# B's output projection in four column groups, and one row of its weights in sixteen transfers

## The chip, the core and the metric

The kernel runs on one core of a Trainium2 chip. The metric is the device time of one execution in microseconds (us), as the median of several runs. A core has four engines that compute (TensorE for matmuls, VectorE, ScalarE, GpSimd) and SyncE, which here only issues transfers. In the profile they are PE (PEld is its weight load), DVE, ACT, POOL and SP. Each engine works through its own list of instructions in order. Transfers (DMA) are issued by SyncE and ScalarE and carried out by sixteen DMA engines beside the computing ones.

## What is computed

Two attention layers for one new token, A and B, with their own inputs, each with 32 heads of 128 and a model width of 512. A looks at the whole cache of 16384 positions, B at its last 4096. For each side:

```python
q = (lambda x, *d: x.transpose(*d))((x @ wq).reshape(B, Sq, Hq, Dh), 0, 2, 1, 3)
...
scores = jnp.einsum("bhqd,bhkd->bhqk", q, k) * (Dh ** -0.5)
p = _softmax(scores, axis=-1)
o = jnp.einsum("bhqk,bhkd->bhqd", p, v)
return (lambda x, *d: x.transpose(*d))(o, 0, 2, 1, 3).reshape(B, Sq, Hq * Dh) @ wo
```

The output is the two results side by side, 1024 numbers in bfloat16: A's 512, then B's 512. The last step, `@ wo`, takes a vector of 4096 (32 heads by 128) to 512.

## The kernel before

Nearly all of the 352 MB read are K and V. The caches are cut into twenty steps, sixteen of two heads of A and four of eight heads of B (B at steps 0, 7, 13 and 19, so the last step is B's). For each step SyncE loads a K tile and a V tile of 8 MB; VectorE multiplies K by q and sums over the 128 elements of a head (`scores_prod`, `scores_tree`); ScalarE does the exponentials; TensorE multiplies the probabilities with V (`pv`) one step later. K has two buffers, V one. The order of the instructions on each engine is the order of the program text (`tc.manual_schedule`), with one loop over the steps (L446) and a hand-written ending (L473 to L489).

The last step's tiles hold other things too. At the last step (L452) a K buffer is taken for A's `wo` (4 MB, L454) and for the first half of the last V (L455); after the loop the V buffer is taken for the second half of the last V (L474) and B's `wo` (L475). `wo` lies in memory as 4096 rows of 512; a partition holds 32 consecutive rows, called r here, of 512 numbers. `load_wo` (L152) loads B's `wo` in five pieces of 16, 8, 4, 3 and 1 of those 32, each over all 128 partitions (L156, L157). All these loads are issued by SyncE, one behind the other.

The ending then runs: A's output vector is turned (`permute_o`), projected with 32 matmuls of 512 columns (`project_out_rows`, L380) and stored from ScalarE's queue (L388). B's last softmax follows, then the two halves of its last V (`pv_columns`, L354, 128 matmuls each), each followed by a product on VectorE (L362); then `permute_o(B)`, which leaves the vector as `OpB`, 128 partitions by 32. `project_out_columns` (L390) has `wo` as the weights: for each piece of the load, each block of 128 output columns and each r one matmul with 128x128 weights and one column of `OpB` as the moving side (L397). The result has the output columns on partitions, one partial sum for each piece and block. VectorE adds the five partial sums (L403), TensorE transposes the 128x4 result (L407), VectorE copies it to bfloat16 (L409), and SyncE stores four rows of 128 (L410).

Each transfer reports its end on a semaphore. The framework hands out eight of these for the queues of SyncE and ScalarE together, in turn, and puts the waits that it takes to be needed ahead of an issue, on the issuing engine.

Of the kernel before, what the change touches and what calls it, by code (L numbers as in the profile page):

```python
# [9 lines left out]
F32 = mybir.dt.float32  # L10
BF16 = mybir.dt.bfloat16
P = 128
ACT = mybir.ActivationFunctionType
ALU = mybir.AluOpType
AX = mybir.AxisListType

HQ, DH = 32, 128
CH = 128
# [7 lines left out]
def kernel(  # L26
# [14 lines left out]
    nc = tc.nc  # L41
# [4 lines left out]
    DN = A_wo.shape[1]  # L46
# [8 lines left out]
    one = ctx.enter_context(tc.tile_pool(name="one", bufs=1))  # L55
    ps_t = ctx.enter_context(tc.tile_pool(name="ps_t", bufs=2, space=bass.MemoryType.PSUM))
    ps_s = ctx.enter_context(tc.tile_pool(name="ps_s", bufs=2, space=bass.MemoryType.PSUM))
# [3 lines left out]
    def kslot(name):  # L61
        return kring.tile([P, 2 * CH, DH], BF16, tag="kring", name=name)

    def vslot(name):
        return vring.tile([P, 2 * CH, DH], BF16, tag="vring", name=name)

    identf = singles.tile([P, P], F32, tag="identf")
# [6 lines left out]
    A, B = _Side(), _Side()  # L74
# [36 lines left out]
    def new_k(T):  # L111
        K[T] = kslot("kt")

    def load_k(T, u=None):
        s, g = steps[T]
        if s is A:
            nc.sync.dma_start(
                out=K[T][:, :, :].rearrange("p l d -> p (l d)"),
                in_=a_pair(A_k_cache, g).rearrange("p l d -> p (l d)"),
            )  # L120
        else:
            for v in (0, 1) if u is None else (u,):
                nc.sync.dma_start(
                    out=K[T][:, v * CH : (v + 1) * CH, :].rearrange("p l d -> p (l d)"),
                    in_=b_window(B_k_cache, 2 * g + v),
                )
# [13 lines left out]
    def load_v_half(T, u, dst):  # L140
        nc.sync.dma_start(  # L141
            out=dst.rearrange("p l d -> p (l d)"), in_=b_window(B_v_cache, 2 * steps[T][1] + u)
        )

    def load_wq(s, W):
        s.wq_t = W
        nc.sync.dma_start(
            out=W.rearrange("p a b -> p (a b)").rearrange("p (c f) -> p c f", c=KC),
            in_=s.wq.rearrange("(p c) f -> p c f", c=KC),
        )  # L150

    def load_wo(s, W, pieces):  # L152
        s.wo_t = W.rearrange("p a b -> p (a b)").rearrange("p (r f) -> p r f", r=HQ)
        src = s.wo.rearrange("(p r) f -> p r f", r=HQ)
        r = 0
        for n in pieces:  # L156
            nc.sync.dma_start(out=s.wo_t[:, r : r + n, :], in_=src[:, r : r + n, :])  # L157
            r += n

    def make_masks(s):  # L160
        nc.vector.tensor_reduce(out=s.mask[:, :], in_=by_head(s, identf[:, :]), axis=AX.X, op=ALU.add)
        n = 8 * s.groups // s.nh
        nc.vector.tensor_copy(
            s.rows[:, :, :, :], s.mask[:, :].unsqueeze(1).unsqueeze(3).broadcast_to([P, n, s.nh, 4])
        )
        for v in range(s.parts):
            w = 32 * s.groups
            block = identf[:, v * w : (v + 1) * w].rearrange("p (g r) -> p r g", g=s.groups)
            nc.vector.tensor_reduce(
                out=s.sel[:, v, :], in_=block[:, 0 : 4 * s.nh, :], axis=AX.X, op=ALU.add  # L170
            )
# [10 lines left out]
    def spread_x(s, flat):  # L182
        s.xb = flat[:, 0 : s.nh * KC * P].rearrange("p (h c m) -> p h c m", h=s.nh, c=KC)
        nc.vector.memset(s.xb, 0.0)
        turn_x(s)
        for j in range(s.nh):
            dst = s.xb[:, j, :, :]
            if s is A:
                dst = dst.rearrange("p c (h i) -> p c h i", h=s.nh)[:, :, j, :]
            else:  # L190
                dst = dst.rearrange("p c (i h) -> p c i h", h=s.nh)[:, :, :, j]
            nc.vector.tensor_copy(dst, s.xT[:, :].unsqueeze(2).broadcast_to([P, KC, P // s.nh]))
# [194 lines left out]
        nc.scalar.copy(row[:, :], ps[:, :])  # L387
        nc.scalar.dma_start(out=out[0, 0:1, 0:DN], in_=row[:, :])  # L388

    def project_out_columns(s, pieces):  # L390
        nf, npc = DN // P, len(pieces)
        ps = ps_s.tile([P, npc, nf], F32, tag="sp", name="out_cols")
        r0 = 0
        for k, n in enumerate(pieces):
            for c in range(nf):
                for r in range(r0, r0 + n):
                    nc.tensor.matmul(  # L397
                        ps[:, k, c : c + 1], lhsT=s.wo_t[:, r, c * P : (c + 1) * P], rhs=s.Op[:, r : r + 1],
                        start=(r == r0), stop=(r == r0 + n - 1),
                    )  # L400
            r0 += n
        cols = one.tile([P, nf], F32, tag="cols", name="cols")
        nc.vector.tensor_reduce(  # L403
            out=cols[:, :], in_=ps[:, :, :].rearrange("p k c -> p c k"), axis=AX.X, op=ALU.add
        )
        pr = ps_t.tile([nf, P], F32, tag="tp", name="out_rows")
        nc.tensor.transpose(pr[:, :], cols[:, :], identf[:, :])  # L407
        rows = one.tile([nf, P], BF16, tag="p", name="rows")
        nc.vector.tensor_copy(rows[:, :], pr[:, :])  # L409
        nc.sync.dma_start(out=out[0, 0, DN : 2 * DN].rearrange("(c f) -> c f", c=nf), in_=rows[:, :])  # L410

    wo_pieces = (16, 8, 4, 3, 1)
    with tc.manual_schedule():
        scratch = kslot("scratch")
        x0 = 4 * KC * P
        for s in (B, A):
            s.x_row = scratch[0:1, :, :].rearrange("p a b -> p (a b)")[:, x0 : x0 + D]
            for a, b in ((0, D // 4), (D // 4, D // 2), (D // 2, D)):
                nc.scalar.dma_start(out=s.x_row[:, a:b], in_=s.x[0, 0:1, a:b])  # L419
            x0 += D  # L420
        new_k(0)
        wqt = vslot("wqt")
        load_wq(B, wqt[:, 0:CH, :])
        load_k(0, 0)
        load_wq(A, wqt[:, CH : 2 * CH, :])
        load_k(0, 1)
        make_identity(nc, identf[:, :])
        nc.vector.memset(one_f[:, :], 1.0)
        nc.vector.memset(one_b[:, :], 1.0)
        nc.vector.memset(ones_col[:, :], 1.0)  # L430
        nc.vector.memset(A.o[:, :], 0.0)
        nc.vector.memset(B.o[:, :], 0.0)
        nc.vector.tensor_copy(ident[:, :], identf[:, :])
        spread_x(B, scratch[:, :, :].rearrange("p a b -> p (a b)"))
        for s in (B, A):
            make_masks(s)
        nc.vector.memset(pick[:, :], 0.0)
        nc.vector.tensor_copy(
            pick[:, 4 : 4 + P].rearrange("h (m k) -> h m k", k=4)[:, :, 0], identf[0:HQ, 0:HQ]
        )  # L440
        spread_x(A, one.tile([P, 2 * KC * P], BF16, tag="o4", name="xbA")[:, :])
        project_q(B)
        project_q(A)
        new_k(1)
        load_k(1)
        for T in range(NT):  # L446
            if T >= 1:
                load_v(T - 1)
                if T + 1 < NT:
                    new_k(T + 1)  # L450
                    load_k(T + 1)
            if T == NT - 1:  # L452
                W = kslot("wot")
                load_wo(A, W[:, 0:CH, :], (HQ,))  # L454
                load_v_half(T, 0, W[:, CH : 2 * CH, :])  # L455
            scores_prod(T, 0)
            if T >= 1:
                un = units[T - 1]
                max_all(un)
                soft(un)  # L460
                spread_p(un)
                soft_sum(un)
                pv(un)
            scores_tree(T, 0)
            if T >= 1:
                recip(un)
                evict(un)
                columns(un)
            scores_prod(T, 1)
            scores_tree(T, 1)  # L470
            if T < NT - 1:
                unit_max(units[T])
        Z = vslot("wot")  # L473
        load_v_half(NT - 1, 1, Z[:, 0:CH, :])  # L474
        load_wo(B, Z[:, CH : 2 * CH, :], wo_pieces)  # L475
        un = units[NT - 1]
        permute_o(A)
        project_out_rows(A)
        unit_max(un)
        max_all(un)  # L480
        soft(un)
        spread_p(un, 0, CH)
        spread_p(un, CH, 2 * CH, nc.vector.tensor_scalar_mul)
        soft_sum(un)
        recip(un)
        pv_columns(un, 0, W[:, CH : 2 * CH, :])
        pv_columns(un, 1, Z[:, 0:CH, :])
        permute_o(B)
        project_out_columns(B, wo_pieces)  # L489


# [28 lines left out]
```

## Time and profile before

| | |
|---|---|
| median of 3 runs | 825.76 us (825.72 to 825.88) |
| span of the profiled execution, first to last instruction | 823.9 us |
| DVE busy | 763.9 us, 93% |
| PE busy | 202.7 us, 25% |
| ACT busy | 60.1 us, 7% |
| moved by DMA | 352.62 MB, mean 428 GB/s |
| chain that ended last, share of DMA | 82% |
| mean granted TensorE clock | 0.592 |

The span is that of the one execution that was profiled; the runs that give the median are timed without a profile and include what lies around the span. The chain that ended last is followed back from the last instruction, at each step to what released it. Times in the profile's views count from the start of the span. "Granted clock" is the share of TensorE's full clock that it was given in a stretch. In the views of instructions a line such as "L397" is a line of the kernel before, and "x16" a number of merged instructions; in the views of waits the columns are the waiting engine and line, what it waited for, us in total, times, and the longest.

### The profile page before, as it was taken

Reading aid. Unit: us, or ns where it says so; the run is one execution under the profiler, and the core shown is the slowest. Engines: PE = TensorE matmul, PEld = TensorE weight load, DVE = VectorE, ACT = ScalarE, POOL = GpSimd, SP = SyncE. Lnnn points to the kernel's source line nnn. Section 1 sums busy time; section 2 is a strip of 40 time slices with the busy share of each in tenths; the row PEclk is TensorE's granted clock in tenths of the full one; section 3 lists DMA queues with packets and bytes.
Section 4 is the critical chain, followed back from the end, with each engine's and each line's share of the span. In section 5 each row is a group of like instructions: output and inputs, shape, how many; then the busy total and the mean of one; then the engine's idle time right before and its main releaser. Section 6 shows DMA issues by size and latency. Waiting matters only on the chain.

```text
span 823.9 us, 4724 instructions
## 1 busy us (share of the span) xinstructions
PE 202.7 (25%) x1985; PEld 100.7 (12%) x1985; DVE 763.9 (93%) x353; ACT 60.1 (7%) x168; POOL 0.7 (0%) x6
## 2 busy tenths in 40 slices
PE   2702212203030303130312213030303020303175
PEld 0201100101010101010101101010101010101035
DVE  2899999999999999999999999999999999999980
ACT  0101000001010000100000000010100000000010
POOL 0000000000000000000000000000000000000000
PEclk9865656565565555565555565565656565556585
DMA  9999999999999999999999999999999999999997
GB/s 384 434 433 433 453 420 443 430 436 440 423 446 420 424 439 443 412 453 420 443 417 449 414 452 410 450 417 428 438 449 424 436 433 430 443 414 445 418 429 296
DMA packets 8107, 352.62 MB, mean 428 GB/s; under 512 B 915, under 2 KB 1046, under 8 KB 1302
## 3 DMA queue, kind: packets, MB, share of 16 engines
q1 hardware_dynamic: 8072, 352.33, 99.2%
q8 instruction: 15, 0.25, 0.1%
q14 instruction: 6, 0.05, 0.0%
q10 hardware_dynamic: 14, 0.00, 0.0%
HBM read 352.32 MB, written 0.00 MB: 428 GB/s over the span
## 4 chain that ended last, share of the span: by engine, by line
DMA 82%; PE 15%; DVE 1%; SPq 0%; issue 0%; ACTq 0%; ACT 0%; DVEq 0%
DMA vt<-in_A_v_cache_dram 65%; DMA vt<-in_B_v_cache_dram 13%; PE oA L331 11%; DMA wot<-in_B_wo_dram 4%; PE oB L331 2%; PE qp L203 2%; DMA scratch<-in_A_x_dram 2%; DVE kt L227 1%; SPq L141 0%; ACTq L419 0%; SPq L157 0%; PE out_cols L397 0%; ACT qB L207 0%; PE out_rows L407 0%; DVE rows L409 0%
## 5 line engine op out<-in xcount | busy, mean ns | idle before, releaser
L233 DVE TENSOR_TENSOR kt<-kt 128x8192 bf16<-128x8192 bf16 (+3 forms) x160 | 344.9, 2156 | 4.8
L227 DVE TENSOR_TENSOR kt<-kt,qA 128x16384 bf16<-128x16384 bf16 x32 | 277.8, 8683 | 11.0 <-DMA kt<-in_A_k_cache_dram 10.9
L331 PE MATMUL oA<-vt,pm 128*8 128x512 bf16 x1024 | 92.3, 538 | 132.1 <-DMA vt<-in_A_v_cache_dram 132.1
L227 DVE TENSOR_TENSOR kt<-kt,qB 128x16384 bf16<-128x16384 bf16 x8 | 69.4, 8680 | 6.3 <-ACT qB L207 6.3
L249 PE MATMUL sm<-identf,m 128*1 128x128 f32 x24 | 8.1, 370 | 227.3 <-DVE m L244 227.3
L331 PEld LDWEIGHTS <-pm 128*8 128x8 bf16 (+1 forms) x1216 | 37.3, 111 | 216.7 <-issue 196.3
L268 PE MATMUL sm<-one_f,Mr 1*128 1x1 f32 x48 | 12.9, 347 | 176.7 <-DVE Mr L264 147.1
L237 DVE TENSOR_REDUCE sc<-kt 128x128 f32<-128x1024 bf16 x40 | 48.8, 1220 | 2.7
L276 ACT ACTIVATE bias<-sm 128x1 f32<-128x1 f32 (+1 forms) x20 | 3.4, 172 | 420.8 <-PE sm L268 420.8
L268 PEld LDWEIGHTS sm<-one_f,Mr 1*128 1x128 f32 x48 | 11.2, 298 | 183.6 <-DVE Mr L264 152.2
L249 PEld LDWEIGHTS sm<-identf,m 128*1 128x1 f32 x24 | 1.7, 79 | 229.3 <-issue 216.2
L340 ACT ACTIVATE o<-oA,r 128x512 f32<-128x512 f32 x16 | 11.0, 688 | 220.5 <-PE oA L331 220.5
L331 PE MATMUL oB<-vt,pm 128*16 128x512 bf16 x192 | 17.2, 494 | 20.3 <-DMA vt<-in_B_v_cache_dram 16.2
L348 PE MATMUL oc<-selA,o 128*128 128x2 f32 x128 | 16.9, 254 | 12.7 <-ACT o L340 12.7
L348 PEld LDWEIGHTS oc<-selA,o 128*128 128x128 f32 x128 | 15.5, 191 | 20.8 <-ACT o L340 20.8
L297 ACT ACTIVATE pm<-p,maskA 128x256 bf16<-128x256 bf16 x32 | 14.5, 500 | 0.5
L315 PE MATMUL sm<-cs,rowsA 128*128 128x1 f32 x32 | 9.4, 362 | 14.3 <-ACT p L282 14.3
L282 ACT ACTIVATE p<-sc,bias 128x256 bf16<-128x256 f32 (+1 forms) x24 | 11.3, 470 | 0.6
L203 PE MATMUL qp<-wqt,xbA 128*128 128x512 bf16 x32 | 8.8, 444 | 6.0 <-DVE kt L227 6.0
L315 PEld LDWEIGHTS sm<-cs,rowsA 128*128 128x128 f32 x32 | 8.0, 310 | 15.7 <-ACT p L282 15.7
L203 PE MATMUL qp<-wqt,scratch 128*128 128x512 bf16 x32 | 9.9, 486 | 0.0
L362 DVE TENSOR_TENSOR OB<-ocol,r 128x4 bf16<-128x4 f32 x2 | 0.3, 161 | 10.2 <-PE ocol L358 10.2
(71 smaller groups left out, 108.1 us busy)
## 6 DMA issues: line engine op xcount, KB each, us to landing
kt<-in_B_k_cache_dram SPq DMA_DIRECT2D x8, 4096.0 KB, 29.1
vt<-in_B_v_cache_dram SPq DMA_DIRECT2D x6, 4096.0 KB, 23.3
wot<-in_B_v_cache_dram SPq DMA_DIRECT2D x2, 4096.0 KB, 22.6
wqt<-in_B_wq_dram SPq DMA_DIRECT2D x1, 4096.0 KB, 12.3
wqt<-in_A_wq_dram SPq DMA_DIRECT2D x1, 4096.0 KB
wot<-in_A_wo_dram SPq DMA_DIRECT2D x1, 4096.0 KB
wot<-in_B_wo_dram SPq DMA_DIRECT2D x1, 2048.0 KB
wot<-in_B_wo_dram SPq DMA_DIRECT2D x1, 1024.0 KB
```

Of the source, the lines that this page charges most:

```text
L203: nc.tensor.matmul(qp[:, :, :], lhsT=s.xb[:, j, c, :], rhs=wq[:, c, j, g : g + 4, :], start=(k == 0), stop=(k == n - 1),)
L227: nc.vector.tensor_tensor(out=k, in0=k, in1=s.q[:, j : j + 1, :].broadcast_to([P, CH, DH]), op=ALU.mult)
L233: nc.vector.tensor_tensor(out=k[:, :, 0:w], in0=k[:, :, 0:w], in1=k[:, :, w : 2 * w], op=ALU.add)
L237: nc.vector.tensor_reduce(out=units[T].sc[:, u * CH : (u + 1) * CH], in_=k[:, :, 0:8], axis=AX.X, op=ALU.add)
L249: nc.tensor.transpose(un.sm[0:1, v * P : (v + 1) * P], m[:, v : v + 1], identf[:, :])
L268: nc.tensor.matmul(un.sm[:, 256 + v : 257 + v], lhsT=Mr[:, v * P : (v + 1) * P], rhs=one_f[:, :], start=True, stop=True,)
L282: nc.scalar.activation(out=un.p[:, v * n : (v + 1) * n], in_=un.sc[:, v * n : (v + 1) * n], func=ACT.Exp, scale=inv, bias=bias[:, v : v + ...
L297: nc.scalar.activation(out=out, in_=in_, func=ACT.Copy, scale=mask)
L315: nc.tensor.matmul(un.sm[v * w : (v + 1) * w, 264:265], lhsT=s.rows[:, :, :, :].rearrange("p r a b -> p (r a b)"), rhs=un.cs[:, v : v + 1] ...
L331: nc.tensor.matmul(s.o[r0 : r0 + un.rows, :], lhsT=un.pm[:, l, :, :].rearrange("p a b -> p (a b)"), rhs=V[un.T][:, 4 * l : 4 * l + 4, :], ...
L340: nc.scalar.activation(out=un.osb[:, :], in_=un.s.o[:, :], func=ACT.Copy, scale=un.r[:, 0:1])
L348: nc.tensor.matmul(oc[:, 0:w], lhsT=un.osb[:, j * P : (j + 1) * P], rhs=sel[:, j, :], start=(j == 0), stop=(j == 3),)
```

## The change

`load_wo` gets an option that is used for B. With it, row r = 0 of the 32 is loaded first and by itself, in sixteen transfers of 15, 14, 13 and so on down to 1 partitions, and a last one of 8 (together 128), each partition 512 numbers or 1 KB. The first big piece is then 15 of the 32 instead of 16. The number of transfers for B's `wo` goes from 5 to 21, all on SyncE's queue, in front of B's store.

`project_out_columns` is replaced by `project_out_groups`. One column of `OpB` is now the weights (128x1) and a 128x128 block of `wo` the moving side; for each r there are four matmuls, one for each block of output columns, which write to partitions 0, 32, 64 and 96 of one PSUM tile and so go to four column groups of TensorE. All 32 r are summed in place. The tile is cleared by VectorE before. The sum over pieces, the transpose and their tiles are gone: one copy of 128x128 to bfloat16 follows, and the store takes the four partitions 0, 32, 64 and 96.

```diff
-    def load_wo(s, W, pieces):
+    def load_wo(s, W, pieces, spread=False):
...
         r = 0
+        if spread:
+            p = 0
+            for k in (*range(15, 0, -1), 8):
+                nc.sync.dma_start(out=s.wo_t[p : p + k, 0, :], in_=src[p : p + k, 0, :])
+                p += k
+            assert p == P
+            r, pieces = 1, (pieces[0] - 1, *pieces[1:])
         for n in pieces:
...
-    def project_out_columns(s, pieces):
-        nf, npc = DN // P, len(pieces)
-        ps = ps_s.tile([P, npc, nf], F32, tag="sp", name="out_cols")
-        r0 = 0
-        for k, n in enumerate(pieces):
+    def project_out_groups(s, pieces):
+        nf = DN // P
+        ps = ps_s.tile([P, P], F32, tag="sp", name="out_groups")
+        nc.vector.memset(ps[:, :], 0.0)
+        for r in range(HQ):
             for c in range(nf):
-                for r in range(r0, r0 + n):
-                    nc.tensor.matmul(
-                        ps[:, k, c : c + 1], lhsT=s.wo_t[:, r, c * P : (c + 1) * P], rhs=s.Op[:, r : r + 1],
-                        start=(r == r0), stop=(r == r0 + n - 1),
-                    )
-            r0 += n
-        cols = one.tile([P, nf], F32, tag="cols", name="cols")
-        nc.vector.tensor_reduce(
-            out=cols[:, :], in_=ps[:, :, :].rearrange("p k c -> p c k"), axis=AX.X, op=ALU.add
-        )
-        pr = ps_t.tile([nf, P], F32, tag="tp", name="out_rows")
-        nc.tensor.transpose(pr[:, :], cols[:, :], identf[:, :])
-        rows = one.tile([nf, P], BF16, tag="p", name="rows")
-        nc.vector.tensor_copy(rows[:, :], pr[:, :])
-        nc.sync.dma_start(out=out[0, 0, DN : 2 * DN].rearrange("(c f) -> c f", c=nf), in_=rows[:, :])
+                nc.tensor.matmul(
+                    ps[32 * c : 32 * c + 1, :], lhsT=s.Op[:, r : r + 1], rhs=s.wo_t[:, r, c * P : (c + 1) * P],
+                    start=(r == 0), stop=(r == HQ - 1),
+                )
+        rows = one.tile([P, P], BF16, tag="p", name="rows")
+        nc.vector.tensor_copy(rows[:, :], ps[:, :])
+        nc.sync.dma_start(
+            out=out[0, 0, DN : 2 * DN].rearrange("(c f) -> c f", c=nf),
+            in_=rows[:, :].rearrange("(c k) f -> c k f", c=nf)[:, 0, :],
+        )
...
-        load_wo(B, Z[:, CH : 2 * CH, :], wo_pieces)
+        load_wo(B, Z[:, CH : 2 * CH, :], wo_pieces, spread=True)
...
-        project_out_columns(B, wo_pieces)
+        project_out_groups(B, wo_pieces)
```

## The prediction

> **What bounds the kernel now.** I read the chain of waits first, and of it only the last 40 us, because every edit lies in the last load and the last projection. Columns: start, length, what.
>
> ```profile
> 787.87 0.54 SPq L141
> 788.41 0.05 issue
> 788.46 0.58 SPq L157
> 789.04 0.05 issue
> 789.10 0.42 SPq L157
> ...
> 790.04 30.16 DMA wot<-in_B_wo_dram
> 820.19 0.04 issue
> 820.24 0.60 PE out_cols L397 x16
> 820.84 0.02 issue
> 820.86 0.19 DVE cols L403
> 821.05 0.04 issue
> 821.09 0.39 PE out_rows L407
> ```
>
> The reader is to see that the end hangs on a transfer: SyncE issues the second half of the last V (L141) at 787.9 and all five pieces of wo (L157) right behind it, and then data flows until 820.19. Only 16 matmuls, a sum, a transpose, a copy and the store come after that. So a microsecond by which wo lands later is a microsecond at the end, and the tail after 820.2 is the only place where arithmetic counts.
>
> Next the waits of the DMA queue itself over that stretch (us in total, times, longest).
>
> ```profile
> SPq L410 <- DVE rows L409: 21.1, 1, 21.1
> ...
> SPq L410 <- DMA wot<-in_B_v_cache_dram: 9.4, 1, 9.4
> ...
> SPq L157 <- DMA wot<-in_A_wo_dram: 0.6, 1, 0.6
> ```
>
> The last two rows look odd, since neither the store (L410) nor a piece of wo (L157) uses what these transfers bring. What they share is a completion semaphore. The list of the built program's SyncE instructions with their semaphores shows eight of them, given out in turn: wo of A has number 6, the first half of the last V 7, A's store 0, the second half 1, the five pieces 2 to 6, and B's store 7 again. A transfer that reuses a number first waits for the transfer that held it: the fifth piece for wo of A (0.6 us), the store for the first half of V (9.4 us, until 791.4 + 9.4 = 800.8). Today these waits cost nothing, because at most five pieces follow.
>
> Last, the DMA issues (KB each, us to landing) and the last stretch in windows (us, PE, PEld, DVE, ACT, POOL busy, granted clock, DMA share, GB/s).
>
> ```profile
> wot<-in_B_v_cache_dram SPq DMA_DIRECT2D x2, 4096.0 KB, 22.6
> wqt<-in_B_wq_dram SPq DMA_DIRECT2D x1, 4096.0 KB, 12.3
> ```
>
> ```profile
> 815.00:816.00 1.00, 0.68 (x20) 0.67 (x20) 0.00 (x0) 0.19 (x1) 0.00 (x0) 0.50 0.97 382
> 816.00:817.00 1.00, 0.42 (x16) 0.34 (x14) 0.00 (x0) 0.00 (x0) 0.00 (x0) 0.50 0.90 356
> 817.00:818.00 1.00, 1.00 (x43) 1.00 (x41) 0.00 (x0) 0.00 (x0) 0.00 (x0) 0.50 0.65 258
> 818.00:819.00 1.00, 1.00 (x39) 0.94 (x36) 0.00 (x0) 0.00 (x0) 0.00 (x0) 0.50 0.51 190
> 819.00:820.00 1.00, 0.61 (x18) 0.50 (x16) 0.00 (x0) 0.00 (x0) 0.00 (x0) 0.50 0.32 116
> ```
>
> A 4096 KB transfer with an empty queue in front of it needs 12.3 us from its issue (wq of B, the kernel's first). Between others it costs only 9.7 us: the first half of V lands at 800.8, the second when PE's wait for it ends, 810.54, and wo's 4096 KB at 820.24. So starting from an empty queue costs 12.3 - 9.7 = 2.6 us. In the windows the DMA share falls from 0.97 to 0.32: the sixteen engines do not finish together, and the last is some 3 us behind the first.
>
> **The change part by part.**
>
> *Sixteen small transfers.* The list for the changed kernel has them ahead of the big pieces, each waiting for the number it takes over. The first five take 2 to 6, as the pieces did (the fifth again waits for wo of A, until 791). The sixth takes 7, held by the first half of V: it waits to 800.8. The seventh takes 0, held by A's store, which is issued at 800.25. The eighth takes 1, held by the second half of V: it can't be issued before 810.5. SyncE issues in order, so behind it stand eight more small transfers, all five big pieces (31 of wo's 32 rows) and B's store. Before, these pieces had been issued since 791 and flowed on without a gap. Now the queue holds nothing but a few rows of row 0 from 810.5 on, and the fast engines run dry about 3 us sooner.
>
> Price of the stall. (a) Nine small issues, the eighth to the sixteenth, before the first big piece. Bounds from the nearest rows: the six x loads on ACT's queue take 1.05 and 0.98 us for three each, or 0.33 to 0.35 us apiece with pauses, the shortest 0.21 + 0.03 = 0.24; the pieces of wo on SyncE stand 0.47 us apart (789.10 to 789.56). Nine cost 2.2 to 4.2 us; I take 0.36 each, since 1 to 9 rows are nearer to an x load (one row) than to 128 rows: 3.25 us. The first big piece starts its issue at 810.55 + 3.25 = 813.8. (b) Starting from empty, 2.6 us, by wq of B. Lower bound: the final store, 0.34 us of issue and 0.6 us until SyncE sees it, together 0.9 (1.0 with pauses). Upper: 2.6 and one instruction fetch on the engine that ends last; the table of DMA queues has 15 such packets taking 0.1% of 16 engines' span, 0.9 us each, so 3.5. (c) Row 0 no longer lies in the stream: 1/32 of 9.7, -0.3 us. Sum: 3.25 + 2.6 - 0.3 = +5.55 us, so the last wait for wo ends near 825.8 instead of 820.24.
>
> The ninth to sixteenth also wait, for the first to eighth small ones. These hide: the first seven land right behind V, and the eighth, issued at 810.55 and landing some 1.0 us later by the store's price, is asked for only eight issues (2.9 us) later. At the 0.24 us pitch it is still 1.9 us. The big pieces wait for small ones issued at least eight issues before, which holds likewise.
>
> The thought that speaks for the small transfers is that they load the 16 engines unevenly and so could level the falling DMA share. They hold 128 KB, 0.3 us of the stream, so even a perfect effect is below a tenth of the stall.
>
> *The matmuls.* Both versions have 128, for 32 rows and four blocks of columns. Before, each had 128x128 weights and one moving column (the largest group of L397: 76 in 2.19 us, 29 ns each). Now each has one column of weights and 128 moving columns, in four groups of TensorE. The row for groups is L331: 128x512 matmuls on four groups, 64 in 5.38 us; in its slow part four weight loads stand every 0.427 us, so four matmuls in 427 ns, while one group alone (L383) gets a single 512-column matmul into the same 0.427 us. At 128 columns that is 107 ns for four, 27 ns each at the half clock that the windows show, and 3.4 us for all. Bounds: 27 ns, and 107 ns if the four do not overlap. I take 27, since L331 has the same interleaving of groups. They are hidden up to a point: the first big piece (15 rows, 15/32 x 9.7 = 4.55 us) lands at 813.8 + 2.6 + 4.55 = 820.95, and from there 120 matmuls fit into the 4.85 us until 825.8 if each takes under 40 ns. After the last wait 16 remain as before: 0.43 against 0.58 us. I count no difference. DVE's memset of the sums comes behind its last product at 814.16 and ahead of the first matmul that needs them, which row 0 and OpB hold to 815.5; a 128x512 memset takes 0.48 us (L431), so it hides.
>
> The page "TensorE: Matmul & The Clock Gate" of the Trainium skill, section "Back-to-back issue gap", gives about 81 ns for each load-and-matmul pair of 128 columns in a stream, and "TensorEngine Tiling (Array Packing)", section "Restrictions", says that column tiling switches the fast weight load off. By the page an estimate of 124 x 81 ns = 10.0 us would follow 820.95. The trace's own pairs are faster (29 ns at L397, 24 in 1.17 us or 49 ns at L331 with 512 columns), so the sum stays with the rows.
>
> *The tail.* Sum (0.19), transpose (0.39) and the pauses between are gone: matmuls end 820.82, the copy starts 821.57, 0.75 us; one hand-over of 0.04 stays. The copy, 128x128 instead of 4x128, has the same 128 elements per partition, so 0.28 us stays (ident, 128x128, took 0.21 at L433). The store still moves four rows of 256 bytes. Its semaphore is now the fourteenth small transfer's, long landed. -0.7 us.
>
> *Sum:* 5.55 - 0.7 = +4.85 us. Against the profiled execution of 823.9 that is 828.75; the median of the runs, 825.76, lies 1.9 above it, so 830.6.
>
> **Rivals.**
>
> *The waits decide nothing* (the other side: not slower). If the eighth small transfer found its number free, all 21 issues would pass while the second half of V flows (22.6 us), and the tail's 0.7 us would be the whole effect: 825.1. It needs A's store and the second half of V to hold other numbers than the list gives; the 9.4 us row speaks against it, as the same reuse is seen waiting there.
>
> *TensorE becomes the bound.* If the four groups do not overlap, 107 ns each: 124 x 0.107 = 13.3 us after 820.95, ending at 834.2 where I have 826.2, so +8.0 more: 838.6. It decides from 40 ns a matmul on. For it: the weights change with every matmul. Against: L331. The page's 81 ns would give 820.95 + 10.0 = 830.95, 835.4, an estimate.
>
> *A's store is the late one.* The seventh waits for it. The x loads on the same queue come to 13.95 us in the chain of waits, from the last issue at 2.51, beside large transfers. A store issued at 800.25 and as late as that would land at 814.2; then ten issues follow, 814.2 + 3.6 = 817.8 instead of 813.8, +4.0: 834.6. Against: six in a row shared that time, 2.3 us apiece, which gives 802.6, well before 810.5.
>
> **How the numbers follow.** The stall as forecast 0.82, TensorE 0.06, A's store 0.06, waits without effect 0.05, and 0.01 for no change. Forecast 830.6. Its own bounds: 2.2 + 1.0 - 0.3 - 0.7 = +2.2, or 828.0; 4.2 + 3.5 - 0.3 - 0.6 = +6.8, or 832.6. The range reaches to the case of A's store, 828.0 to 834.6; the case faster and the slow TensorE are left out. Differences under 0.2% (1.7 us) count as no change, about what a measurement of this kernel can tell. The 0.05 of the case at 825.1, which lies inside that band, go 0.02 to faster, should the tail gain more, and 0.03 to no change: faster 0.02, same 0.04, slower 0.94.
>
> **What would show it.** SyncE's waits: a small transfer waiting about 9.7 us for the second half of V, ending at 810.5, and the first big piece issued near 813.8. Windows: the DMA share near zero between 811 and 815, then high to about 825. The chain: nine issues on SyncE's queue and one DMA after them ahead of the last matmuls. L397's successor: four matmuls about every 107 ns. The tail: copy right behind the last matmul. The forecast is wrong if the big pieces are issued before 810, if the DMA share does not fall, or if the matmuls go on for microseconds after the last landing.

## The result and the profile after

The changed kernel takes 831.98 us (median of 4 runs, 831.81 to 832.58) against 825.75; the ratio of the two is 1.0077, its 95% interval 1.0063 to 1.0091. The profiled execution's span is 830.0 us against 823.9, so 6.1 us longer. Lines of the changed kernel stand a little further down: the small transfers are L159, the big pieces of wo L164, the matmuls L403, the copy L408, B's store L409.

The chain of waits of the changed kernel over its end (start, length, what):

```profile
787.43 22.97 DMA wot<-in_B_v_cache_dram
...
810.42 0.27 SPq L159
...
810.74 0.29 SPq L159
...
813.32 0.36 SPq L164
...
814.66 11.78 DMA wot<-in_B_wo_dram
...
826.48 0.65 PE out_groups L403 x15
```

Before, the chain went from the issue of the fourth piece at 790.04 straight to the data. Now SyncE stands in the middle of it: the second half of the last V lands at 810.41, and only then does the eighth small transfer go out, with eight more behind it, 0.32 us apart, and the first big piece of wo at 813.32. The waits of SyncE's queue name what it stood for (us in total, times, longest):

```profile
SPq L159 <- DMA wot<-in_B_v_cache_dram: 12.2, 2, 9.4
...
SPq L159 <- DMA out_dram<-row: 6.5, 1, 6.5
...
SPq L159 <- DMA wot<-in_A_wo_dram: 1.0, 1, 1.0
```

None of these brings anything that a transfer of wo uses. By the list of the built program they held the semaphores 6, 7, 0 and 1: wo of A (the fifth small transfer), the two halves of V (the sixth, 9.4 us, and the eighth, 12.2 - 9.4 = 2.8 us), and between them A's store (the seventh, 6.5 us). The eighth's wait is this short only because the two before it had already used up the time: SyncE stood at the sixth to 800.6 and at the seventh to 807.3. That a store of ScalarE's queue is among those waited for fits semaphores that both queues share, and speaks against a limit of SyncE's queue alone.

What the data did meanwhile, in windows (us, PE, PEld, DVE, ACT, POOL busy, granted clock, DMA share, GB/s):

```profile
805.00:807.00 2.00, 1.65 (x62) 1.65 (x62) 0.02 (x1) 0.30 (x2) 0.00 (x0) 0.50 0.70 292
807.00:809.00 2.00, 1.90 (x72) 1.82 (x69) 0.06 (x1) 0.00 (x0) 0.00 (x0) 0.50 0.62 242
809.00:811.00 2.00, 0.55 (x20) 0.55 (x21) 0.10 (x1) 0.00 (x0) 0.00 (x0) 0.50 0.04 13
811.00:813.00 2.00, 2.00 (x81) 2.00 (x79) 0.00 (x0) 0.00 (x0) 0.00 (x0) 0.50 0.09 25
...
823.00:824.00 1.00, 0.73 (x28) 0.54 (x21) 0.00 (x0) 0.00 (x0) 0.00 (x0) 0.50 1.02 402
824.00:825.00 1.00, 0.59 (x16) 0.40 (x16) 0.00 (x0) 0.00 (x0) 0.00 (x0) 0.50 0.66 234
825.00:826.00 1.00, 0.00 (x0) 0.00 (x0) 0.00 (x0) 0.00 (x0) 0.00 (x0) 0.50 0.05 17
```

From 809 to 813 the DMA engines carry next to nothing (13 and 25 GB/s). Their share is down from 805 on already, to 0.70 and 0.62, where the kernel before has 0.96 and 0.95: behind V only a few rows stand in the queue, and the engines that finish V early find nothing to do. The second thing to see is at the end: after 825 the share is 0.05, about one engine of sixteen. By that share fifteen are done, and TensorE waits until 826.48 for the one that is left.

### The profile page after: what moved, and what is told of

Its sections match the earlier page's. It is cut to its first block, busy times and chain, and to the rows that moved or that the text cites. A ratio compares the mean times of both kernels' runs of the same rounds, so it can differ in the third digit from the quotient of the medians.

```text
span 830.0 us, 4742 instructions
## 1 busy us (share of the span) xinstructions
PE 206.3 (25%) x1984; PEld 101.3 (12%) x1984; DVE 764.0 (92%) x353; ACT 60.1 (7%) x168; POOL 0.7 (0%) x6
## 4 chain that ended last, share of the span: by engine, by line
DMA 84%; PE 14%; SPq 1%; issue 0%; DVE 0%; DVEq 0%
DMA vt<-in_A_v_cache_dram 64%; DMA vt<-in_B_v_cache_dram 13%; PE oA L338 11%; DMA wqt<-in_A_wq_dram 4%; DMA wot<-in_B_v_cache_dram 3%; PE oB L338 2%; DMA wot<-in_B_wo_dram 1%; PE qp L210 1%; SPq L159 0%; SPq L141 0%; DMA scratch<-in_B_x_dram 0%; SPq L164 0%; PE out_groups L403 0%; DVE rows L408 0%; DVEq L408 0%
## 5 line engine op out<-in xcount | busy, mean ns | idle before, releaser
L275 PE MATMUL sm<-one_f,Mr 1*128 1x1 f32 x48 | 12.9, 348 | 176.7 <-DVE Mr L271 146.8
L338 PE MATMUL oB<-vt,pm 128*16 128x512 bf16 x192 | 19.6, 555 | 20.3 <-DMA vt<-in_B_v_cache_dram 16.2
L408 DVE CAST rows<-out_groups 128x128 bf16<-128x128 f32 x1 | 0.3, 292 | 12.8 <-PE out_groups L403 12.8
L390 PE MATMUL out_row<-wot,OpA 128*1 128x512 bf16 x32 | 9.9, 486 | 0.5 <-DMA wot<-in_A_wo_dram 0.5
```

Of the source, the lines that this page charges most:

```text
L275: nc.tensor.matmul(un.sm[:, 256 + v : 257 + v], lhsT=Mr[:, v * P : (v + 1) * P], rhs=one_f[:, :], start=True, stop=True,)
L338: nc.tensor.matmul(s.o[r0 : r0 + un.rows, :], lhsT=un.pm[:, l, :, :].rearrange("p a b -> p (a b)"), rhs=V[un.T][:, 4 * l : 4 * l + 4, :], ...
L390: nc.tensor.matmul(ps[:, :], lhsT=s.Op[:, r : r + 1], rhs=s.wo_t[:, r, :], start=(r == 0), stop=(r == HQ - 1))
```

## The experiments

The theory was the forecast's: the eighth transfer behind the second half of V takes over that half's semaphore and holds up everything behind it. The rivals: the projection in column groups costs the time; the small transfers cost it by themselves, each a share. Each ratio below is to the kernel before, timed beside the run; its median was 825.75 to 825.94 us throughout.

**The parts alone.** The column groups without the small transfers, and the small transfers with the old projection:

```diff
-        load_wo(B, Z[:, CH : 2 * CH, :], wo_pieces, spread=True)
+        load_wo(B, Z[:, CH : 2 * CH, :], wo_pieces)
```

> The projection in column groups alone, wo in its five pieces as before, no small transfers. Theory 1 (SyncE waits for a semaphore that the second half of V still holds): no stall, big pieces issued by 791.5, last wait for wo near 820.2. The tail after that wait was 1.64 us to the store's issue before and 1.04 in the changed kernel, but the store itself and the end took 0.45 us longer there, so 825.5 to 825.9. Rival, the projection costs the time itself: about 832. Also open: whether the store's issue takes 0.34 us as before or 0.63 as in the changed kernel; 0.63 here would put it on the store's four spread partitions.

```diff
-        project_out_groups(B, wo_pieces)
+        project_out_columns(B, wo_pieces)
```

> The sixteen small transfers alone, projection by columns as before. Theory 1: the whole stall, big piece issued near 813.3, last wait near 826.4, then the old tail of 1.64 us: 831.9 to 832.6. Rival, the projection costs the time: 825.8. Rival, the two only cost together (TensorE falls behind): between the two.

The groups alone take 825.62 us, ratio 0.9998 (0.9990 to 1.0007); run once more, 825.64, ratio 0.9997 (0.9988 to 1.0006). The small transfers alone take 832.2, ratio 1.0078 (1.0064 to 1.0092). The whole loss is the transfers', and the projection is not to be told from no change. In the trace of the small transfers alone the first big piece is issued at 813.55 and the last wait ends at 826.84, as in the changed kernel.

The trace of the groups alone shows why their gain does not reach the end (timeline: start, us, engine, line, operation):

```profile
820.43 0.60 PE L403 MATMUL out_groups<-wot,OpB 128*1 128x128 bf16 x16 [0.39 <-DMA wot<-in_B_wo_dram]
...
821.13 0.29 DVE L408 CAST rows<-out_groups 128x128 bf16<-128x128 f32 x1 [6.28 <-PE out_groups L403]
821.46 0.66 SPq L409 DMA_DIRECT2D out_dram<-rows  x1
```

From the last wait to the store's issue it is now 821.46 - 820.43 = 1.03 us, against 1.64 in the kernel before. But the issue itself takes 0.66 us. The small transfers alone, with the old store from four neighbouring partitions, need 0.29 for it, the kernel before 0.34. The price is the spread partitions'. It takes back half of the 0.61 us; the rest goes into a last wait that ended 0.19 us later (820.43 against 820.24) and 0.1 us more behind the issue, and both spans are 823.9 us.

In the second trace of the groups alone it is not wo that ends last, but TensorE:

```profile
817.87 3.15 PE L403 MATMUL out_groups<-wot,OpB 128*1 128x128 bf16 x109 [1.11 <-issue]
```

These matmuls run to 821.02 without a wait for wo, behind an idle 1.11 us for which the profile names no releaser. So without the stall the new projection has little time to spare; what the idle time is was not tried.

**Seven and six transfers.** Only the number and size of the small transfers for row 0 is changed:

```diff
-            for k in (*range(15, 0, -1), 8):
+            for k in (16, 16, 16, 16, 16, 16, 32):
```

> Row 0 in seven transfers (six of 16 partitions, one of 32) instead of sixteen, the rest as changed. Theory 1: the first big piece is now the eighth transfer and takes the semaphore of the second half of V itself; it is issued at 810.5 instead of 813.3, so 2.9 us less than the changed kernel: 829.1, and the start from an empty queue (some 2.5 to 3.5 us with the late fetch) is what remains against before. Rival, each small transfer costs a share of its own (6.2 us for sixteen): 825.75 + 7/16 x 6.2 = 828.5.

```diff
-            for k in (*range(15, 0, -1), 8):
+            for k in (16, 16, 16, 16, 16, 48):
```

> Row 0 in six transfers (five of 16 partitions, one of 48). Theory 1: the first big piece is the seventh transfer, waits only for A's store near 807, and lies in the queue before the second half of V has landed; only the 8-row piece and what follows wait to 810.5, with 4.6 us of data ahead of them. No stall: 825.4 to 826.0, 3 us less than with seven. Rival, a share for each small transfer: 825.75 + 6/16 x 6.2 = 828.1, 0.4 us less than with seven.

Seven take 829.43 us (ratio 1.0045, 1.0032 to 1.0057), six 826.21 (1.0006, 0.9997 to 1.0015), 0.2 above what was expected: 3.2 us for one transfer. A share for each would have made that step 0.4 us. SyncE's waits in the trace with seven:

```profile
SPq L159 <- DMA wot<-in_B_v_cache_dram: 9.4, 1, 9.4
...
SPq L159 <- DMA out_dram<-row: 6.3, 1, 6.3
SPq L164 <- DMA wot<-in_B_v_cache_dram: 2.9, 1, 2.9
```

The wait for the second half of V has moved from a small transfer (L159) to the first big piece (L164), which goes out at 810.62. With six the first big piece is issued at 806.28 and only the second waits, to 811.05, with 1.9 MB in front of it: the windows from 805 to 815 never fall below a share of 0.87. The cliff lies exactly where the numbering puts it.

**Twice as many.** Rows 0 and 1 in sixteen each:

```diff
-            p = 0
-            for k in (*range(15, 0, -1), 8):
-                nc.sync.dma_start(out=s.wo_t[p : p + k, 0, :], in_=src[p : p + k, 0, :])
-                p += k
-            assert p == P
-            r, pieces = 1, (pieces[0] - 1, *pieces[1:])
+            for r in (0, 1):
+                p = 0
+                for k in (*range(15, 0, -1), 8):
+                    nc.sync.dma_start(out=s.wo_t[p : p + k, r, :], in_=src[p : p + k, r, :])
+                    p += k
+                assert p == P
+            r, pieces = 2, (pieces[0] - 2, *pieces[1:])
```

> The changed kernel with rows 0 and 1 in sixteen small transfers each, 32 in all, and a first big piece of 14 rows. Theory 1: behind the eighth stand 25 small issues instead of 9, each 0.32 us as in the changed kernel: +5.15, less 0.3 for the row taken out of the stream: 836.8. Rival, the stall is one wait of fixed length, however many issues stand behind it: 832. Rival, each small transfer costs a share of 6.2/16 us: 838.2.

837.61 us, ratio 1.0143 (1.0129 to 1.0157). The wait of fixed length falls (832). The theory is 0.8 low, a share for each 0.6 high; the time alone does not tell these two apart. The trace does: the eighth small transfer goes out at 810.82, when V's second half is in, the first big piece at 819.36, and the last wait ends at 832.25, 12.9 us after that, as with sixteen (13.2). So the 25 issues took 8.54 us, 0.34 each, against 0.32 with nine, which is 0.5 us more, and V's half came 0.4 us later: about the 0.8. The added loss is issue time in front of the first big piece.

**The same transfers without the wait.** GpSimd's queue has semaphores of its own:

```diff
-                nc.sync.dma_start(out=s.wo_t[p : p + k, 0, :], in_=src[p : p + k, 0, :])
+                nc.gpsimd.dma_start(out=s.wo_t[p : p + k, 0, :], in_=src[p : p + k, 0, :])
```

> The changed kernel with the same sixteen small transfers, issued on GpSimd's queue, which has semaphores of its own; SyncE issues only the five big pieces, with the semaphores 2 to 6 as before. Theory 1: no stall although the sixteen transfers are all there, last wait for wo near 820.2, 825.3 to 826.0, as with the column groups alone (825.62). Rival, the small transfers or their uneven load on the engines cost the time: 829 to 832.

826.99 us, ratio 1.0014 (1.0005 to 1.0024): between the two, and outside both expectations. SyncE issues all five big pieces by 791.7 and the stall is gone, 5 of the 6.2 us. What remained was first put down to row 0. GpSimd reuses its semaphores too, each small transfer from the ninth on waits 1.4 to 3.0 us for an older one, and the last is issued at 811.71; all 128 matmuls then run behind it (818.79, 3.58 us). So row 0 was taken last:

```diff
-        for r in range(HQ):
+        for r in (*range(1, HQ), 0):
...
-                    start=(r == 0), stop=(r == HQ - 1),
+                    start=(r == 1), stop=(r == 0),
```

> The sixteen small transfers on GpSimd's queue as in the run before (826.99), but the matmuls take row 0 last instead of first. Theory: what was left there against 825.62 was row 0, landing at 818.66 on the other queue with all 128 matmuls (28 ns each, 3.58 us) behind it; with row 0 last TensorE works off the other rows as they land and four to sixteen matmuls follow the last wait, so about 0.3 to 0.5 us less, 826.5 to 826.7, and the rest of the difference is that the big pieces themselves land later, beside the small ones. Rival, the small transfers cost nothing in the stream: 825.6. Rival, the order of the rows decides nothing: 827.0.

827.2 us, ratio 1.0015 (1.0006 to 1.0024). That explanation falls: taking row 0 last gains nothing. The other half of the expectation holds, that the big pieces land later beside the small ones. The timeline of this run:

```profile
812.04 3.57 PE L365 MATMUL ocol<-pm,wot 128*128 128x4 bf16 x128 [3.27 <-DMA wot<-in_B_v_cache_dram]
...
821.68 0.91 PE L403 MATMUL out_groups<-wot,OpB 128*1 128x128 bf16 x20 [0.41 <-DMA wot<-in_B_wo_dram]
```

The second half of V is waited for until 812.04 (811.79 in the run before it), against 810.5 to 810.9 in the four traces without small transfers, and wo until 821.68 against 820.43 with the groups alone: the stream as a whole is 1.2 us late. That is most of the 1.6 us between 827.2 and the 825.64 of the groups alone. Another 0.3 us lie behind the last wait, where 20 matmuls stand instead of 16 (1.33 us to the store's issue against 1.03). The windows from 791 to 809, first of this run, then of the groups alone on the same chip:

```profile
791.00:809.00 18.00, 14.17 (x168) 7.40 (x167) 10.11 (x14) 3.17 (x12) 4.25 (x9) 0.78 1.00 408
```

```profile
791.00:809.00 18.00, 14.63 (x168) 7.71 (x167) 10.34 (x14) 3.17 (x12) 0.00 (x0) 0.69 1.00 430
```

The run before has 409 GB/s there, and all four traces without small transfers 427 to 430. Small transfers that run beside the stream all the time slow it; why was not tried.

**Levelling the engines.** The 3-row piece split into 125 and 3 partitions, on the column groups alone:

```diff
         for n in pieces:
-            nc.sync.dma_start(out=s.wo_t[:, r : r + n, :], in_=src[:, r : r + n, :])
-            r += n
+            for p, q in ((0, 125), (125, P)) if n < 0 else ((0, P),):
+                nc.sync.dma_start(out=s.wo_t[p:q, r : r + abs(n), :], in_=src[p:q, r : r + abs(n), :])
+            r += abs(n)
...
-    wo_pieces = (16, 8, 4, 3, 1)
+    wo_pieces = (16, 8, 4, -3, 1)
```

> Column groups alone, with the 3-row piece of wo split into 125 and 3 partitions; after the rule that a transfer goes to as many of the lowest-numbered engines as divide its partitions evenly, 125 go to five engines (25 rows each instead of 8) and the other eleven get that much less at the end. If the five lowest engines are among those that end 3 us early (windows of the kernel before: DMA share falling from 0.97 to 0.32 over its last 4 us): eleven engines have 24 KB less, 0.9 us at 27 KB per us, so 824.7 against 825.62 with the column groups alone. If an engine among those five is one of the late ones: it gets 51 KB more, +1.9 us, 827.5. If the rule doesn't hold here: 825.6.

828.62 us, ratio 1.0034 (1.0022 to 1.0047): slower, by 1.1 us more than the worst case. Its last windows:

```profile
820.00:821.00 1.00, 0.20 (x12) 0.20 (x15) 0.00 (x0) 0.00 (x0) 0.00 (x0) 0.50 0.27 78
821.00:822.00 1.00, 0.39 (x16) 0.18 (x5) 0.00 (x0) 0.00 (x0) 0.00 (x0) 0.50 0.10 39
822.00:823.00 1.00, 0.00 (x0) 0.00 (x0) 0.00 (x0) 0.00 (x0) 0.00 (x0) 0.50 0.06 24
```

After 820 about four engines (0.27 of sixteen) are busy, then two, then one. A few engines did get the rows, and they were not the ones with time to spare. The rule behind it is in the Trainium skill, page "DMA: Bandwidth & Descriptors", section "Why a DMA increments its semaphore by 16 and not by 1" (the largest count up to 16 that divides the partitions, on the lowest-numbered engines); the share of 0.27 after 820, four to five engines, agrees with the five that the rule gives for 125 partitions, but no view here names an engine. Without knowing which engines are late there is nothing to level.

**The one late engine.** In the changed kernel the 8-row and the 4-row piece are waited for until 822.71 and 824.02, and then the 3-row piece until 826.48, 2.46 us for 0.9 us of data (3/32 x 9.7). The table of DMA queues over 823.3 to 826 has one packet on the instruction queue, 0.02 MB, taken here to be a fetch of instructions. A shorter program was to do without it: two groups of 256 columns, 64 matmuls.

```diff
-        nf = DN // P
-        ps = ps_s.tile([P, P], F32, tag="sp", name="out_groups")
+        nf, W2 = 2, DN // 2
+        ps = ps_s.tile([P, W2], F32, tag="sp", name="out_groups")
...
-                    ps[32 * c : 32 * c + 1, :], lhsT=s.Op[:, r : r + 1], rhs=s.wo_t[:, r, c * P : (c + 1) * P],
+                    ps[64 * c : 64 * c + 1, :], lhsT=s.Op[:, r : r + 1], rhs=s.wo_t[:, r, c * W2 : (c + 1) * W2],
...
-        rows = one.tile([P, P], BF16, tag="p", name="rows")
+        rows = one.tile([P, W2], BF16, tag="p", name="rows")
```

> The changed kernel with two column groups of 256 columns instead of four of 128: 64 matmuls instead of 128, so TensorE's program is 64 load-and-matmul pairs shorter at its end. It tells apart why the 3-row piece of wo was waited for until 826.48 in the changed kernel, 1.5 us later than its neighbours let expect. Theory A, a 16 KB instruction fetch (one packet of the instruction queue between 823.3 and 826) pushes one of the sixteen engines back: the shorter program no longer needs that fetch, no instruction packet from 815 on, last wait near 825.1; then sixteen pairs become eight at about 107 ns, some 0.9 us, so 831.0. Theory B, the late engine comes from the transfers themselves: last wait again near 826.4, 832.2. Beside it: the store has two partitions now; an issue of 0.63 us again would put its price on partitions apart, not on their number.

832.54 us, ratio 1.0079 (1.0065 to 1.0093). Its table of DMA queues from 815 to 828 has (queue, kind: packets, MB, share):

```profile
q8 instruction: 1, 0.02, 0.5%
```

The fetch was there all the same, and so was a late engine: the DMA share falls to 0.08 at 826 and TensorE waits for wo until 827.61. The run does not decide. It took longer than either theory said, 832.2 at most, because one thing went otherwise than in the changed kernel: a small transfer issued at 811.13 took 3.4 us to land, and the first big piece, which takes over its semaphore, waited 0.8 us for it and went out at 814.53. The forecast took such waits to be hidden, and in the changed kernel they were.

The other traces say more about the late engine. In all four with sixteen or more small transfers on SyncE, the last instruction packet starts shortly before the others end (near 823.6 in the changed kernel, 824.1 with the old projection, 829.6 with thirty-two, 825.1 with two groups), and then the share stays at 0.02 to 0.08 for one to two microseconds. With seven small transfers a packet starts near 815.6, while the first big piece is loading. There it is this piece that is late: it is waited for until 8.60 us after its issue, against 6.7 to 7.0 in the four, and the last wait ends only 0.97 us after the one before; a second packet, near 822.4, adds nothing that shows. From the issue of the first big piece to the last wait it is 12.9 to 13.4 us in all five. So in these five the lost time goes with a fetch that falls into the loading of wo; no run took the fetch away.

The store's issue took 0.61 us with two partitions, so its price is that they lie apart, not how many they are.

## Why the prediction was right, and where it was off

Forecast were 830.6 us, in a range of 828.0 to 834.6; measured are 831.98. The mechanism was right: the eighth transfer, the semaphore of V's second half, SyncE in order behind it, an empty queue. The parts alone, the step from six to seven transfers and the same transfers on GpSimd's queue show it. By the steps, in us:

| step | forecast | measured |
|---|---|---|
| V's second half in, counted from the last wait before, 820.24 | 810.55 - 820.24 = -9.7 | 810.42 - 820.24 = -9.8 |
| nine small issues, to the first big piece | 3.25 | 813.32 - 810.42 = 2.90 |
| first big piece, issue to the last wait for wo | 825.8 - 813.8 = 12.0 | 826.48 - 813.32 = 13.16 |
| last wait to the store's issue | -0.7 | 1.04 against 1.64: -0.60 |
| store's issue to the end of the span | 0 | 830.0 - 827.52 = 2.48, before 823.9 - 821.88 = 2.02: +0.46 |
| sum, span | +4.85 | +6.1 |

The sum is 1.25 us short. The first two steps came out 0.5 us shorter than forecast and hid part of what the later ones missed.

- *The issues.* They stood 0.32 us apart instead of 0.36, next to the x loads (0.33 to 0.35) that the forecast went by.
- *The empty queue.* This term missed by most. Worked out as in the forecast, 13.16 us less 9.4 for 31 rows, it was 3.8 us, against 2.6 taken and an upper bound of 3.5. The start itself was sized well: the first big piece was waited for until 820.20, 6.88 us after its issue, forecast 2.6 + 4.55 = 7.15. The term fell short at its end, by one engine. The bound named such a fetch on the engine that ends last (+0.9) but the value taken left it out. The fetch and the lost time stand together in the five traces above; that the one causes the other is argued, not shown. What fits it: before, the engines ended up to 3 us apart, and in the flowing stream an engine with time to spare could take a fetch. After the start from empty the share fell from 1.02 to 0.05 within two microseconds (823 to 825), so the others ended close together, and whichever is held up is the last.
- *TensorE.* Hidden, as forecast: 60 matmuls in 1.77 us behind the first big piece, 29.5 ns each at a granted clock of 0.50, and 28 ns in the run where all 128 follow one another (3.58 us). Forecast 27, against 107 without overlap of the groups. The estimate from the 81 ns of the Trainium skill, page "TensorE: Matmul & The Clock Gate", section "Back-to-back issue gap", is not what these groups of one weight column show.
- *A's store.* It was late: it held the seventh transfer for 6.5 us, to 807.3, which is 5.8 us after its own issue at 801.50. The 2.3 us that the forecast set against this rival, the x loads' time divided by six, were too few. But it landed 3.1 us before V's second half, so the rival did not come about. Because of it the eighth waited 2.8 us and not the 9.7 that were named as the sign; the end of that wait, 810.4, was as forecast.
- *The tail.* The gain was sized well and counted as if it reached the end. "The store still moves four rows of 256 bytes" was true and not enough: its issue went from 0.34 to 0.63 us, the step that was left out of the sum.

## What to carry to other kernels

Count the transfers behind a long one: where completion semaphores are handed out in turn, one transfer too many waits for the long one and stops its whole queue, and every issue behind that wait is paid one by one. Such a wait costs nothing as long as enough data stands in the queue ahead of it, as the run with six shows. A wait in the profile for something that the waiting instruction does not use is the sign, even where it costs nothing today. A gain in a last step has to be followed to the last instruction, through the issue of the final store.

## What the runs showed of the hardware

- A store from partitions that lie 32 or 64 apart took 0.61 to 0.66 us to issue on SyncE in all ten traces with the column groups, one from four neighbouring partitions 0.29 and 0.34 in two.
- With small transfers on GpSimd's queue beside it the full stream ran at 408 and 409 GB/s over 18 us, against 427 to 430 in four traces without them, and wo came 1.2 us late.
- In the four traces with sixteen or more small transfers on SyncE about one engine of sixteen was still at work one to two microseconds after the others (share 0.02 to 0.08), each time behind one instruction packet (0.02 MB, 6 to 7% of sixteen engines' microsecond, so about 1 us on one of them). That the fetch is the cause is not shown.
